# Sending 48 of 2048 softmax score units to VectorE in a two-layer attention and GLU kernel

## The chip, the cores and the metric

The kernel runs on one core of a Trainium2 chip. The metric is the device time of one execution in microseconds; the median of several runs counts. TensorE is called PE, VectorE DVE, ScalarE ACT, GpSimd POOL and SyncE SP, as the profile names them.

## The reference

Two layers of the same two blocks with the same weights, on one sequence of 2048 tokens of width 448. Attention has 16 heads of width 28; the gated block has an inner width of 1792. All arrays are float32.

```python
def _A_ref(x, wqkv, wo):                      # attention
    qkv = (x @ wqkv).reshape(B, S, 3, H, Dh).transpose(2, 0, 3, 1, 4)
    q, k, v = qkv[0], qkv[1], qkv[2]
    scores = einsum("bhqd,bhkd->bhqk", q, k) * (Dh ** -0.5)
    p = softmax(scores, axis=-1)
    o = einsum("bhqk,bhkd->bhqd", p, v)
    return o.transpose(0, 2, 1, 3).reshape(B, S, D) @ wo

def _B_ref(x, w_gate, w_up, w_down):          # gated linear unit
    return (sigmoid(x @ w_gate) * (x @ w_up)) @ w_down

x = A_x
for layer in range(2):
    x = x + _A_ref(layernorm(x), A_wqkv, A_wo)
    x = x + _B_ref(layernorm(x), B_w_gate, B_w_up, B_w_down)
```

## The kernel before

The program is written for one order: the tile framework's own scheduling is off, so every engine executes its instructions in the order in which the Python code issues them. Semaphores are put in where one engine reads what another wrote, or where a buffer is used again. Each layer has four stages: `project` (queries, keys, values), `attend`, `out_project` and `gated`.

The change is in `attend`. Its work is cut into *units*. A unit is one block of 128 keys (`kc`, 16 of them per head) against one block of 512 queries (`qb`, 4 of them). So a head has 64 units, four to a chunk of keys, and a layer has 1024.

- `score(g)` takes the three units of group g. PE writes 3 x 4 matmuls (line 821) into one of two accumulators of three banks each (`triple(g % 2)`); the four matmuls of a unit each fill 32 of the 128 partitions and run side by side. I call these four a *quad*. One ACT instruction (line 828) then takes the exponentials of all 3 x 512 columns into a buffer `prob`, out of a ring of five. A group may start only when ACT has read the group that used the same accumulator, two groups earlier.
- `mix(i)` multiplies half of the queries of one chunk's four units with the values (line 839) and adds them up in `acc`, one bank per head (`bank(h % 2)`). It is two quads on PE. Two of them make up a chunk.
- `finish(h)` runs after a head's last `mix`. DVE copies `acc` out (line 853), spreads and inverts the sum of the exponentials (854, 855), multiplies (856) and splits the result in two halves of 16 bits (857, 858); SP sends it on by DMA (line 871).
- `more(g)` scores group g, and at a head's unit 8 issues the operands of the head after next: a memset on DVE (line 442) and six DMAs on SP.

The loop at the end of `attend` sets PE's order. After each group it lets one or two calls of `mix` follow, alternately, if their exponentials are at least two groups old:

```python
for g in range(2, groups + 3):
    more(g)
    for _ in range(1 + g % 2):
        if i < halves and (NB * (i // 2) + 3) // 3 <= g - 2:
            mix(i)
```

In layer 0 this loop also runs `Prepare`, one step every six chunks: it reads the weights of the later stages, measures them (line 742) and splits them on DVE (lines 183 and 188), and writes them back. Its reads, its writes, the heads' operands and the heads' outputs all go through SP's one queue.

The banks of the accumulators are all in use: two triples, and `bank0` and `bank1` for `acc`. While head h adds up in one of these two, the other holds the sum of head h-1 until line 853 has copied it, and then nothing until head h+1 begins.

Of the kernel before, what the change touches and what calls it, by code (L numbers as in the profile page):

```python
# [11 lines left out]
F32 = mybir.dt.float32  # L12
BF16 = mybir.dt.bfloat16
F16 = mybir.dt.float16
I32 = mybir.dt.int32
AF = mybir.ActivationFunctionType
ALU = mybir.AluOpType
AX = mybir.AxisListType

P = 128  # L20
S = 2048
D = 448
H = 16
DH = 28
F = 1792
NT = S // P
NB = 4
TB = NT // NB
W = TB * P
# [10 lines left out]
VC = 32  # L40
SLACK = 1.0201
GUARD_LIMIT = 56.0

N_SLOTS = 19
N_QUART = 12
# [38 lines left out]
def interleaved_layers(ctx: ExitStack, tc: tile.TileContext, x_in, wqkv, wo, w_gate, w_up,  # L84
                       w_down, out):
    nc = tc.nc
    ctx.enter_context(tc.manual_schedule())

    cpool = ctx.enter_context(tc.tile_pool(name="cpool", bufs=1))
# [4 lines left out]
    qrt = Slots(spool, "q", N_QUART)  # L94
# [4 lines left out]
    def new_banks():  # L99

        if banks["stack"] is not None:
            banks["stack"].close()
        uid[0] += 1
        banks["stack"] = ExitStack()
        banks["pool"] = banks["stack"].enter_context(
            tc.tile_pool(name=f"psum{uid[0]}", bufs=1, space=bass.MemoryType.PSUM,
                         reuse_waits="tile"))

    def psum(tag, name, shape):
        uid[0] += 1  # L110
        return banks["pool"].tile(shape, F32, name=f"{name}_{uid[0]}", tag=tag, bufs=1)

    def triple(i, name):
        return psum(f"triple{i}", name, [P, 3, 512])

    def bank(i, name):
        return psum(f"bank{i}", name, [P, 512])
# [16 lines left out]
    back = cpool.tile([P, 4], F32, name="back")  # L134
# [70 lines left out]
    def both_back(i, a, b, by):  # L205

        e = pw.bitcast(F32)
        nc.vector.scalar_tensor_tensor(back[:, i:i + 1], e[:, a:a + 1], by * 2.0 ** 128,
                                       e[:, b:b + 1], op0=ALU.mult, op1=ALU.mult)
# [172 lines left out]
    class WeightsQKV:  # L382
# [32 lines left out]
        def keep(self):  # L415
            for i in range(2):
                nc.sync.dma_start(qk_parts[i], self.qk[i])
            nc.sync.dma_start(v_parts, self.v)
            big.put(*self.qk, self.v)
# [36 lines left out]
            big.put(self.both)  # L456

    exp_scale = nc.scalar.alloc_register("exp_scale")
    gate_scale = nc.scalar.alloc_register("gate_scale")

    def run_fill(fill, n=1):
# [5 lines left out]
    def project(layer, wq, first):  # L467
# [136 lines left out]
        if layer > 0:  # L604
            big.put(*wq.qk)
        else:
            both_back(0, 0, 1, SCALE * 2.0 ** -20)
            nc.scalar.reg_load(exp_scale, back.bitcast(I32)[0:1, 0:1])

        heads = [HeadOperands(0), HeadOperands(1)]  # L610
        top = cpool.tile([H, 2], F32, name=f"top{layer}", tag="top", bufs=1)
# [20 lines left out]
        def worst_of_heads():  # L632
            pb = bank(4, "bounds")
            nc.tensor.matmul(pb[0:1, 0:H], bnd, ident[0:H, 0:H], start=True, stop=True)
            nc.vector.tensor_reduce(worst, pb[0:1, 0:H], axis=AX.X, op=ALU.max)
            nc.vector.tensor_scalar(flag, worst, back[0:1, 0:1], GUARD_LIMIT / 2, op0=ALU.mult,
                                    op1=ALU.is_gt)
# [162 lines left out]
    def attend(layer, values, heads, last_values, gate, keep):  # L800
        new_banks()
        heads = list(heads)
        outs = Outputs()
        prepare = None
        ring = big.ring(5)
        total = H * NT
        units = total * NB
        probs, accs = {}, {}

        def score(g):  # L810

            ps = triple(g % 2, "sc")
            prob = big.at(ring, "prob", [P, 3, W])
            us = range(3 * g, min(3 * g + 3, units))
            for a, u in enumerate(us):
                c, qb = u // NB, u % NB
                h, kc = c // NT, c % NT
                hd = heads[h]
                for j in range(4):
                    keys = slice(kc * P + 32 * j, kc * P + 32 * j + 32)  # L820
                    nc.tensor.matmul(ps[32 * j:32 * j + 32, a, :], hd.k[:, keys],  # L821
                                     hd.q[:, qb * W:(qb + 1) * W], start=True, stop=True,
                                     tile_position=(0, 32 * j))
                probs[u] = prob[:, a, :]
                if u % (NT * NB) == NT * NB - 1:
                    hd.drop()
            n = len(us)
            nc.scalar.activation(prob[:, 0:n, :], ps[:, 0:n, :], AF.Exp, scale=exp_scale)  # L828

        def mix(i):  # L830

            c, n = i // 2, slice(i % 2 * 256, i % 2 * 256 + 256)
            h, kc = c // NT, c % NT
            if kc == 0 and i % 2 == 0:
                accs[h] = bank(h % 2, "acc")
            acc = accs[h]
            v = values[kc // TB]
            for qb in range(NB):
                nc.tensor.matmul(acc[qb * VC:(qb + 1) * VC, n], v[:, kc % TB, h, :],  # L839
                                 probs[c * NB + qb][:, n], start=(kc == 0 and i % 2 == 0),  # L840
                                 stop=(kc == NT - 1 and i % 2 == 1), tile_position=(0, qb * VC))
            if i % 2:
                for qb in range(NB):
                    probs.pop(c * NB + qb)
                if kc == NT - 1:
                    finish(h)

        def finish(h):
            acc = accs.pop(h)
            raw = qrt.get("oraw", [P, W])  # L850
            den = qrt.get("oden", [P, W])
            hl = qrt.get("ohl", [P, 2, W], F16)
            nc.vector.tensor_copy(raw, acc)  # L853
            nc.vector.stream_shuffle(den, raw, [DH] * 32)
            nc.vector.reciprocal(den, den)  # L855
            nc.vector.tensor_tensor(raw, raw, den, op=ALU.mult)
            nc.vector.tensor_copy(hl[:, 0, :], raw)
            nc.vector.tensor_tensor(hl[:, 1, :], raw, hl[:, 0, :], op=ALU.subtract)
            r, end = h * DH, (h + 1) * DH
            while r < end:  # L860
                kt, p = r // P, r % P
                n = min(P - p, end - r)
                if kt == len(outs.kt):
                    outs.grow()
                o = outs.kt[kt]
                other = nc.scalar if h == H - 1 else nc.sync
                for qb in range(NB):
                    e = qb * VC + r - h * DH
                    c = slice(qb * W, (qb + 1) * W)
                    if kt < 3:  # L870
                        nc.sync.dma_start(o[p:p + n, :, c], hl[e:e + n])
                    else:
                        nc.sync.dma_start(o[p:p + n, c], hl[e:e + n, 0, :])
                        other.dma_start(o[64 + p:64 + p + n, c], hl[e:e + n, 1, :])
                r += n
            qrt.put(raw, den, hl)

        groups = (units + 2) // 3

        def more(g):  # L880
            if g >= groups:
                return
            for u in range(3 * g, 3 * g + 3):
                if u % (NT * NB) == 8:
                    h = u // (NT * NB)
                    if h + 2 < H:
                        hd = HeadOperands(h + 2)
                        heads.append(hd)
                        hd.load()
                        hd.load_guard()  # L890
                    elif h == H - 1:
                        gate.load_out()
                        gate.load_gu()
            score(g)

        for g in range(2):
            more(g)
        last_values()
        halves, i = 2 * total, 0
        for g in range(2, groups + 3):  # L900
            more(g)

            for _ in range(1 + g % 2):
                if i < halves and (NB * (i // 2) + 3) // 3 <= g - 2:
                    mix(i)
                    i += 1
                    c = i // 2 - 1
                    if i % 2:
                        continue
                    if layer == 0 and c == 2:  # L910
                        keep()
                    if layer == 0 and c == 4:
                        prepare = Prepare()
                    if prepare and prepare.steps and c > 4 and c % 6 == 0:
                        prepare.steps.popleft()()
        assert i == halves
        big.put(*values)
        big.free.extend(ring)
        return outs
# [160 lines left out]
    for layer in range(LAYERS):  # L1080
        values, heads, last_values = project(layer, wq, first)
        gate = WeightsGated()
        outs = attend(layer, values, heads, last_values, gate, wq.keep)
        mlp_first = out_project(outs, gate)
        wq = WeightsQKV()

        def before_next(f, wq=wq):
            if f == 6:
                wq.load()

        first = gated(layer, mlp_first, gate, before_next)
# [28 lines left out]
```

## Time and profile before

| | |
|---|---|
| runs | 2023.3, 2023.67, 2027.02 us; median 2023.67 |
| profiled execution | 2026.13 us, its span 2024.2 us, mean granted clock 0.998 |
| PE busy | 2005.5 us (99%) |
| ACT busy | 1189.6 us (59%) |
| DVE busy | 748.8 us (37%) |
| POOL busy | 33.3 us (2%) |
| `attend`, layer 0 | from about 128.9 to 591.2 us |
| `attend`, layer 1 | from about 1129.0 to 1590.9 us |

The busy time of PE is a union of intervals with modelled ends: matmuls overlap each other in it, so 99% doesn't say that PE can't go faster. ACT is busy all through the two `attend` stages and little elsewhere. In the rows of the profile, "x" is the number of instructions, and the two numbers behind the bar are the busy time in microseconds and the mean duration of one in nanoseconds.

### The profile page before, as it was taken

How to read it: one execution, taken by the hardware profiler on the slowest of the kernel's cores; microseconds unless marked ns; L12 is line 12 of the kernel's file. 1: busy time of each engine (PE TensorE's matmuls, PEld its weight loads, DVE VectorE, ACT ScalarE, POOL GpSimd, SP SyncE). 2: the span in 40 equal slices, each digit the busy share in tenths (PEclk: the TensorE clock that was granted, in tenths of full speed). 3: DMA queues.
4: the chain of work that ended last, by engine and by line, in shares of the span. 5: the costliest groups of instructions: out<-in, count | busy, mean ns of one | idle time of the engine just before them, and what ended most of it. 6: DMA issues, size and time to landing. Idle time of an engine off the chain costs nothing. (4 is left out here: it accounts for less than half of the span.)

```text
span 2024.2 us, 47829 instructions
## 1 busy us (share of the span) xinstructions
PE 2005.5 (99%) x21637; PEld 1028.8 (51%) x21637; DVE 748.8 (37%) x1110; ACT 1189.6 (59%) x1136; POOL 33.3 (2%) x75
## 2 busy tenths in 40 slices
PE   8999999999999999999999999999999999999999
PEld 4445555555554444444444555555555544444444
DVE  6635455551235232323274133222322432323222
ACT  5469999999961212121244799999999412121211
POOL 2000000000000000000000000000000000000000
PEclk9999999999999999999999999999999999999999
DMA  4563454741215100001143221121202250101000
GB/s 164 156 195 96 130 157 147 227 131 30 57 59 188 37 13 25 19 19 33 59 130 120 66 66 34 42 46 30 66 12 63 68 204 1 55 1 55 1 19 19
DMA packets 98630, 153.75 MB, mean 76 GB/s; under 512 B 9584, under 2 KB 79216, under 8 KB 95600
## 3 DMA queue, kind: packets, MB, share of 16 engines
q1 hardware_dynamic: 89728, 146.21, 23.9%
q10 hardware_dynamic: 8688, 4.36, 0.8%
q8 instruction: 174, 2.85, 0.6%
q14 instruction: 40, 0.33, 0.1%
HBM read 97.52 MB, written 45.68 MB: 71 GB/s over the span
## 5 line engine op out<-in xcount | busy, mean ns | idle before, releaser
L828 ACT ACTIVATE prob_s<-sc 128x1536 f32<-128x1536 f32 (+1 forms) x684 | 918.2, 1509 | 2.6 <-PE sc L821 1.4
L839 PE MATMUL acc<-prob_s,val_s 128*32 128x256 f32 x8192 | 571.7, 379 | 0.0
L821 PE MATMUL sc<-qp_s 114*32 114x512 f16 x8192 | 569.8, 380 | 1.5 <-ACT val_s L537 1.3
L362 PEld LDWEIGHTS <-gu_s 128*128 128x128 f16 x2464 | 241.1, 98 | 290.4 <-issue 6.4
L839 PEld LDWEIGHTS acc<-prob_s,val_s 128*32 128x32 f32 x8192 | 273.6, 110 | 179.8 <-ACT prob_s L828 0.4
L821 PEld LDWEIGHTS <-qp_s 114*32 114x32 f16 x8192 | 245.8, 95 | 222.3 <-issue 75.8
L362 PE MATMUL gate<-xhl_s,gu_s 128*128 128x512 f16 x1232 | 285.1, 379 | 4.2 <-ACT xhl_s L172 2.6
L362 PE MATMUL up<-xhl_s,gu_s 128*128 128x512 f16 x1232 | 284.2, 379 | 0.0
L1028 ACT ACTIVATE sig_q<-gate 128x512 f32<-128x512 f32 x112 | 66.9, 597 | 341.0 <-PE gate L362 324.8
L1033 DVE SCALAR_TENSOR_TENSOR sig_q<-up,sig_q 128x512 f32<-128x512 f32 x112 | 77.5, 692 | 460.9 <-PE up L362 460.9
L172 ACT CAST hhl_q<-sig_q 128x512 f16<-128x512 f32 x112 | 69.3, 618 | 288.1 <-DVE sig_q L1033 288.1
L853 DVE COPY oraw_q<-acc 128x512 f32<-128x512 f32 x32 | 22.1, 692 | 484.5 <-PE acc L839 484.4
L999 PE MATMUL dnp<-dn_s,hhl_q 128*128 128x448 f16 x448 | 157.9, 352 | 0.0
L998 PE MATMUL dnp<-dn_s,hhl_q 128*128 128x448 f16 x448 | 157.9, 352 | 0.0
L1000 PE MATMUL dnp<-dn_s,hhl_q 128*128 128x448 f16 x448 | 157.9, 352 | 0.0
L362 PE MATMUL qkp<-xhl_s,wqk_s 128*128 128x512 f16 x616 | 140.8, 380 | 0.9 <-DVE xhl_s L178 0.7
L855 DVE RECIPROCAL oden_q<-oden_q 128x512 f32<-128x512 f32 x32 | 107.3, 3353 | 1.1
L173 DVE TENSOR_TENSOR hhl_q<-sig_q,hhl_q 128x512 f16<-128x512 f32 x112 | 77.5, 692 | 76.7 <-ACT hhl_q L172 76.7
L362 PEld LDWEIGHTS <-wqk_s 128*128 128x128 f16 x616 | 57.2, 98 | 71.7 <-issue 4.5
L506 ACT ACTIVATE qkhl_q<-qkp 128x512 f16<-128x512 f32 x56 | 33.4, 596 | 65.5 <-PE qkp L362 65.4
L999 PEld LDWEIGHTS <-hhl_q 128*128 128x128 f16 x448 | 43.8, 98 | 43.8
L998 PEld LDWEIGHTS <-hhl_q 128*128 128x128 f16 x448 | 43.8, 98 | 43.8
(113 smaller groups left out, 1034.8 us busy)
## 6 DMA issues: line engine op xcount, KB each, us to landing
qp_s<-qk_scr SPq DMA_DIRECT2D x96, 224.0 KB
qk_scr<-qkhl_q SPq DMA_DIRECT2D x56, 256.0 KB
gu_s<-gu_parts SPq DMA_DIRECT2D x14, 1024.0 KB
xraw_s<-xt_scr SPq DMA_DIRECT2D x14, 768.0 KB
xt_scr<-xs_s SPq DMA_DIRECT2D x38, 224.0 KB
qp_s<-qk_scr SPq DMA_DIRECT2D x64, 112.0 KB
gu_parts<-pack_s SPq DMA_DIRECT2D x7, 1024.0 KB
raw_s<-in_B_w_down_dram SPq DMA_DIRECT2D x6, 896.0 KB
```

What stands on the lines that cost most here:

```text
L172: nc.scalar.copy(hi, raw)
L173: nc.vector.tensor_tensor(lo, raw, hi, op=ALU.subtract)
L362: nc.tensor.matmul(pm, w, x, start=(i == 0), stop=(i == len(terms) - 1))
L821: nc.tensor.matmul(ps[32 * j:32 * j + 32, a, :], hd.k[:, keys], hd.q[:, qb * W:(qb + 1) * W], start=True, stop=True, tile_position=(0, 32 ...
L828: nc.scalar.activation(prob[:, 0:n, :], ps[:, 0:n, :], AF.Exp, scale=exp_scale)
L839: nc.tensor.matmul(acc[qb * VC:(qb + 1) * VC, n], v[:, kc % TB, h, :], probs[c * NB + qb][:, n], start=(kc == 0 and i % 2 == 0), stop=(kc ...
L855: nc.vector.reciprocal(den, den)
L998: nc.tensor.matmul(pm, hl[:, 0, s], dw[:, 0, :], start=(f == 0), stop=False)
L999: nc.tensor.matmul(pm, hl[:, 0, s], dw[:, 1, :], start=False, stop=False)
L1000: nc.tensor.matmul(pm, hl[:, 1, s], dw[:, 0, :], start=False, stop=(f == NF - 1))
L1028: nc.scalar.activation(sig, pgu[0], AF.Sigmoid, scale=gate_scale)
L1033: nc.vector.scalar_tensor_tensor(sig, pgu[1], PS, sig, op0=ALU.mult, op1=ALU.mult)
```

## The change

In each head, one unit in layer 0 and two units in layer 1 are left out of the groups. Over the kernel that is 16 + 32 = 48 of 2048 units. Each is scored by itself (`score_aside`), ahead of its chunk: into the bank that will be the next head's `acc`, just before the group that holds the first unit of chunk 3 (or of chunk 8, for the second one of layer 1). Ten DVE instructions turn its scores into exponentials as powers of two: multiply by the scale and log2(e) and clamp, add a constant to round, subtract to get the fraction, a polynomial of degree five, a shift of the rounded number into the exponent, and the product. The unit's chunk is 15 in layer 0; in layer 1 it is 10 for the first and 15 for the second.

The groups of three are formed from the units that are left: 336 in layer 0 and 331 in layer 1, where there were 342 in each. The loop that places `mix` is written anew: it goes on while the chunk's last group is at least two groups old and while a proportional pace allows it.

```diff
+        side = {}
+        for h in range(H):
+            for at, kc, qb in ((3, 15, 1),) if layer == 0 else ((3, 10, 3), (8, 15, 1)):
+                side[(h * NT + at) * NB] = (h * NT + kc) * NB + qb
+        main = [u for u in range(units) if u not in side.values()]
+        groups = (len(main) + 2) // 3
+        last_group = {u // NB: n // 3 for n, u in enumerate(main)}
...
-            us = range(3 * g, min(3 * g + 3, units))
+            us = main[3 * g:3 * g + 3]
...
+        def score_aside(u):
+            ps = bank(1 - u // (NT * NB) % 2, "aside")
+            scores(ps, u)
+            y = qrt.get("expo", [P, W])
+            t = qrt.get("whole", [P, W])
+            p = qrt.get("power", [P, W])
+            c = POWER_OF_2
+            nc.vector.tensor_scalar(y, ps, base2[:, 0:1], -126.0, op0=ALU.mult, op1=ALU.max)
+            nc.vector.tensor_scalar(t, y, ROUND, None, op0=ALU.add)
+            nc.vector.scalar_tensor_tensor(y, t, ROUND, y, op0=ALU.subtract, op1=ALU.subtract)
+            nc.vector.tensor_scalar(p, y, c[5], c[4], op0=ALU.mult, op1=ALU.add)
+            nc.vector.tensor_tensor(p, p, y, op=ALU.mult)
+            for k in (3, 2, 1):
+                nc.vector.scalar_tensor_tensor(p, p, c[k], y, op0=ALU.add, op1=ALU.mult)
+            whole = t.bitcast(I32)
+            nc.vector.tensor_scalar(whole, whole, 23, None, op0=ALU.logical_shift_left)
+            nc.vector.scalar_tensor_tensor(p, p, c[0], t, op0=ALU.add, op1=ALU.mult)
...
         def more(g):
             if g >= groups:
                 return
-            for u in range(3 * g, 3 * g + 3):
+            for u in main[3 * g:3 * g + 3]:
+                if u in side:
+                    score_aside(side[u])
...
-            for _ in range(1 + g % 2):
-                if i < halves and (NB * (i // 2) + 3) // 3 <= g - 2:
-                    mix(i)
-                    i += 1
+            while (i < halves and last_group[i // 2] <= g - 2
+                   and (g >= groups or i * groups < halves * (g - 1))):
+                mix(i)
+                i += 1
```

`scores(ps, u)` is the old inner loop of `score`, now a function: four matmuls into a given bank.

More of the change, by code (lines that the diff above doesn't have):

```diff
@@ L42 @@
 GUARD_LIMIT = 56.0
+POWER_OF_2 = (1.0000001192092896, -0.6931469440460205, 0.24022120237350464,
+              -0.05550713464617729, 0.009675540030002594, -0.0013276454992592335)
+ROUND = 12583039.0
 N_SLOTS = 19
@@ L458, in interleaved_layers @@
     exp_scale = nc.scalar.alloc_register("exp_scale")
+    base2 = cpool.tile([P, 1], F32, name="base2")
     gate_scale = nc.scalar.alloc_register("gate_scale")
@@ L608, in project @@
             nc.scalar.reg_load(exp_scale, back.bitcast(I32)[0:1, 0:1])
+            nc.vector.tensor_scalar(base2, back[:, 0:1], math.log2(math.e), None, op0=ALU.mult)
         heads = [HeadOperands(0), HeadOperands(1)]
@@ L808, in attend, with scores @@
         probs, accs = {}, {}
+        side = {}
[5 more added lines that the diff above has]
+        last_group = {u // NB: n // 3 for n, u in enumerate(main)}
+        def scores(ps, u):
+            c, qb = u // NB, u % NB
+            hd, kc = heads[c // NT], c % NT
+            for j in range(4):
+                keys = slice(kc * P + 32 * j, kc * P + 32 * j + 32)
+                nc.tensor.matmul(ps[32 * j:32 * j + 32, :], hd.k[:, keys],
+                                 hd.q[:, qb * W:(qb + 1) * W], start=True, stop=True,
+                                 tile_position=(0, 32 * j))
         def score(g):
@@ L813, in score @@
             prob = big.at(ring, "prob", [P, 3, W])
-            us = range(3 * g, min(3 * g + 3, units))
+            us = main[3 * g:3 * g + 3]
             for a, u in enumerate(us):
[L816 to L823, printed above, removed]
+                scores(ps[:, a, :], u)
                 probs[u] = prob[:, a, :]
                 if u % (NT * NB) == NT * NB - 1:
-                    hd.drop()
+                    heads[u // (NT * NB)].drop()
             n = len(us)
             nc.scalar.activation(prob[:, 0:n, :], ps[:, 0:n, :], AF.Exp, scale=exp_scale)
+        def score_aside(u):
[15 more added lines that the diff above has]
+            nc.vector.scalar_tensor_tensor(p, p, c[0], t, op0=ALU.add, op1=ALU.mult)
+            qrt.put(y, t)
+            probs[u] = p
+            aside.append(u)
+        aside = []
         def mix(i):
@@ L843, in mix @@
                 for qb in range(NB):
-                    probs.pop(c * NB + qb)
+                    p = probs.pop(c * NB + qb)
+                    if c * NB + qb in aside:
+                        qrt.put(p)
                 if kc == NT - 1:
@@ L876, in finish @@
             qrt.put(raw, den, hl)
-        groups = (units + 2) // 3
         def more(g):
@@ L901, in attend @@
             more(g)
-            for _ in range(1 + g % 2):
-                if i < halves and (NB * (i // 2) + 3) // 3 <= g - 2:
-                    mix(i)
-                    i += 1
[L907 to L915, printed above, removed]
+            while (i < halves and last_group[i // 2] <= g - 2
+                   and (g >= groups or i * groups < halves * (g - 1))):
+                mix(i)
+                i += 1
+                c = i // 2 - 1
+                if i % 2:
+                    continue
+                if layer == 0 and c == 2:
+                    keep()
+                if layer == 0 and c == 4:
+                    prepare = Prepare()
+                if prepare and prepare.steps and c > 4 and c % 6 == 0:
+                    prepare.steps.popleft()()
         assert i == halves
```

## The prediction

> **What bounds the kernel now.** I read the page first, then the busy time by stretches, then the timeline of single engines inside `attend`.
>
> ```profile
> PE 2005.5 (99%) x21637; PEld 1028.8 (51%) x21637; DVE 748.8 (37%) x1110; ACT 1189.6 (59%) x1136; POOL 33.3 (2%) x75
> L828 ACT ACTIVATE prob_s<-sc 128x1536 f32<-128x1536 f32 (+1 forms) x684 | 918.2, 1509 | 2.6 <-PE sc L821 1.4
> ```
>
> PE looks full and ACT half idle. The busy time by stretches corrects this for the two `attend` stages (columns: PE, PEld, DVE, ACT, POOL, granted clock, DMA share, GB/s):
>
> ```profile
> 128.90:591.20 462.30, 462.14 (x8204) 260.38 (x8204) 196.04 (x220) 459.72 (x343) 0.45 (x1) 1.00 0.42 123
> 1129.00:1590.90 461.90, 461.77 (x8204) 260.25 (x8204) 122.75 (x120) 459.57 (x343) 0.00 (x0) 1.00 0.18 43
> ```
>
> There ACT is busy for 459.7 of 462.3 us. Which of the two really waits, the timeline shows:
>
> ```profile
> 398.55 14.95 ACT L828 ACTIVATE prob_s<-sc 128x1536 f32<-128x1536 f32 x11
> ...
> 401.24 2.86 ACT L828 ACTIVATE prob_s<-sc 128x1536 f32<-128x1536 f32 x2
> ...
> 401.63 0.84 PE L821 MATMUL sc<-qp_s 114*32 114x512 f16 x12
> 402.28 0.62 PE L839 MATMUL acc<-prob_s,val_s 128*32 128x256 f32 x8
> 402.81 0.83 PE L821 MATMUL sc<-qp_s 114*32 114x512 f16 x12
> 403.45 1.05 PE L839 MATMUL acc<-prob_s,val_s 128*32 128x256 f32 x16
> 404.31 0.84 PE L821 MATMUL sc<-qp_s 114*32 114x512 f16 x12
> ```
>
> Eleven exponentials in 14.95 us with a last one of 1.52 give (14.95 - 1.52) / 10 = 1.343 us per group. PE repeats two groups in 404.31 - 401.63 = 2.68 us, the same pace. In it, every quad takes 0.215 us (404.31 - 403.45 for four), twelve make 2.59, and the rest is one gap: eight mixing matmuls (two quads, 0.44) start at 402.28, and the scores follow only at 402.81. They waited for the ACT instruction that began at 401.24 and ended 1.52 later, at 402.76. So ACT bounds `attend`, but PE is behind it by just 0.09 us in 2.69, or 3.4%.
>
> Three more durations matter. Scores start 0.05 us after ACT has left their accumulator. When ACT is dry, it starts 0.05 after the last score (the third group's scores end at 133.37, ACT stands idle and starts at 133.42) and needs 1.45:
>
> ```profile
> 133.42 1.45 ACT L828 ACTIVATE prob_s<-sc 128x1536 f32<-128x1536 f32 x1 [0.23 <-DMA qp_s<-qk_scr]
> ```
>
> So a dry ACT ends a group 1.50 after its scores; a fed one ends them 1.343 apart.
>
> **The change part by part.**
>
> *Units taken from ACT.* 48 units are 16 groups: 16 x 1.343 = 21.5 us less on ACT (7.2 in layer 0, 14.3 in layer 1).
>
> *DVE's ten instructions.* Nearest rows in layer 0's `attend`:
>
> ```profile
> L858 DVE TENSOR_TENSOR ohl_q<-oraw_q,ohl_q 128x512 f16<-128x512 f32 x15 | 10.4, 692 | 0.5
> L857 DVE CAST ohl_q<-oraw_q 128x512 f16<-128x512 f32 x15 | 6.4, 427 | 0.5
> ```
>
> Seven like the first (two tensors, or from an accumulator) and three like the second (one tensor and constants): 7 x 0.69 + 3 x 0.43 + gaps of 0.03 = 6.4 us; 7.2 if none is like the second. DVE has room: in layer 1 a head's 28.6 us hold `finish` (6.8), a memset (1.8, some 0.5 of waiting) and two of these, 21.9. The tightest use is layer 1's chunk 10. Its power is there about 6.8 + 2.3 + 6.4 = 15.5 us after the last head's copy started; it is mixed ten chunks, 18 us, after. Nothing waits, by 2 to 3 us; the cost is zero.
>
> *PE.* The same quads, in another order. The listing of the changed program shows it. Write S for a group's scores (three quads), M for a whole chunk of mixing (two `mix`, four quads). Before, it runs S M S m (m is half). After, both halves of a chunk become ready at once and the pace never splits them: S S M S M S M, four groups to three chunks. S and M together take 404.31 - 402.81 = 1.51, more than ACT's 1.343, and S S only 0.65. So PE falls behind ACT over three groups and then meets the wait for an accumulator, though the averages are the same. With two accumulators the loop is this. The second S of a pair starts; three S M later (3 x 1.51 = 4.53) the last S of the run starts, its scores end 0.83 later, ACT is dry and ends them 1.50 after that. Three more groups at 1.343 (4.03), 0.05, and the second S of the next pair but one may start: 4.53 + 0.83 + 1.50 + 4.03 + 0.05 = 10.94 us for eight groups, where ACT alone needs 8 x 1.343 = 10.74. Loss: 0.20 per eight groups, 0.525 per head of 21 groups (layer 0), 0.517 per head of 20.67 (layer 1).
>
> To this come, per head, the aside quads (0.215 each, one or two) and runs of five groups with four M instead of three (one per head in layer 0, two in layer 1), each 1.51 - 1.343 = 0.17: at most 0.385 and 0.77, at least nothing where they fall into the half of the loop that runs on ACT. I carried the durations above through the written order of a head: PE starts at the later of its last end and the accumulator's release, ACT ends at the later of its last end + 1.343 and the scores + 1.50. That gives 0.27 and 0.57, so 0.79 and 1.09 us per head in all. Layer 0: 16 x 0.79 - 7.2 = +5.5. Layer 1: 16 x 1.09 - 14.3 = +3.1. Bounds: +1.2 to +7.4 and -6.1 to +6.3.
>
> *The wait for the bank.* Aside scores go to the bank of the last head's sum, so PE now waits for line 853. Between a head's last mixing and the next head's aside, PE has S, S, M (2.2 us; in layer 1 at times S, M, 1.5). The copy mostly ends 0.76 after the last mixing: free. But not behind `Prepare` in layer 0:
>
> ```profile
> 358.55 0.75 DVE L183 TENSOR_SCALAR pack_s<-raw_s,up 128x1024 f16<-128x1024 f32 x1 [10.72 <-DMA dn_parts<-pack_s]
> ...
> 366.00 0.75 DVE L183 TENSOR_SCALAR pack_s<-raw_s,up 128x1024 f16<-128x1024 f32 x1 [3.39 <-DMA raw_s<-in_B_w_gate_dram]
> ...
> 370.53 1.76 DVE L442 MEMSET qp_s<- 18x2048 f16 x1 [0.47 <-issue]
> 372.32 0.69 DVE L853 COPY oraw_q<-acc 128x512 f32<-128x512 f32 x1
> ```
>
> DVE stands in its queue for two DMAs, and the copy of head 7 ends at 373.01, 9.2 us after its last mixing (363.77). Nobody waited; now everything behind PE's aside does. In the changed listing the memset stands behind the copy (1.8 sooner), and head 7 takes 0.35 longer while the DMAs hang on head 6's output: 7.1 late, less 2.2, so PE stands for 4.9 us and ACT with it. Head 8's copy was as late (9.5) but hangs by SP's queue on head 7's output, and PE now comes 4.9 + 0.35 later and the memset goes behind it too: no further wait. The cost: 4.9, from 0 (the DMAs land sooner) to 6.6 (the memset gains nothing).
>
> A PE that stands can also lose clock. The start of the trace shows it: PE idle from 6.95 to 10.08 us, then
>
> ```profile
> 5.00:9.70 4.70, 1.95 (x6) 0.56 (x4) 1.10 (x3) 1.55 (x1) 0.19 (x1) 1.00 1.02 345
> 9.80:16.50 6.70, 5.56 (x22) 4.27 (x23) 4.55 (x14) 2.76 (x6) 5.17 (x15) 0.50 1.09 339
> ```
>
> half the clock for 6.7 us. That would cost half of 6.7, 3.4 us, once; I leave it out of the sum, as 4.9 us is a single wait between dense work, and keep it in the range. The Trainium skill (TensorE: Matmul & The Clock Gate, "What's actually happening") says that one idle window of about 3.4 us, on a free-running count, halves the clock; this trace agrees (3.13 us idle, 0.50). By that rule the wait would hold a whole window about four times in ten, and the sum would then be 3.4 us higher.
>
> *Edits with one answer.* `base2` is one small DVE instruction per kernel; qrt buffers and `last_group` cost nothing; other stages are untouched. Loads of the head after next sit behind `finish` by up to 7 us, with a head (28 us) to spare.
>
> **Sum.** +5.5 + 3.1 + 4.9 = +13.5 us: the profiled execution would go from 2026.13 to 2039.6, the median, 2.5 lower, from 2023.67 to 2037.2.
>
> **The rivals.**
> 1. *ACT stays the bound.* If the runs of three S M are absorbed, the whole 21.5 us show: 2002.2, or 2007.1 with the bank wait. For it: PE has 3.4% to spare on average. Against: 10.94 > 10.74. It decides at 0.20 us per loop: a dry ACT that finished in 1.30 rather than 1.50, or an M shorter by 0.07. Chance 0.13.
> 2. *The loop costs but the aside quads hide and the DMAs land in time:* +1.2 - 6.1 = -4.9, 2018.8; with part of the bank wait about unchanged, near 2021 to 2027. Chance 0.13.
> 3. *DVE falls behind.* In layer 0's heads 3 to 9 the powers push `Prepare` back 6.4 us each, and more copies come late, each by some 5 us: with four, 3 x 4.9 more, 2052. For it: DVE and SP wait for each other there. Against: in the other heads DVE stood idle for 0.8 to 10 us before the copy. Chance 0.12.
>
> That the units do not leave ACT isn't a rival: the listing has 667 exponentials of groups.
>
> **How the numbers follow.** The forecast (loop, most of the quads, one bank wait) has 0.62. A measurement of this kernel tells about 0.2%, 4 us, from no change. Faster: rival 1 and the low end of rival 2, 0.16. Same: the rest of rival 2 and the low end of the forecast, 0.13. Slower: 0.71. The forecast's own bounds are 2018.8 to 2023.67 + 7.4 + 6.3 + 6.6 = 2044; with half clock 2047, and part of rival 3 up to 2050. The range 2018 to 2050 leaves out rival 1 and the top of rival 3.
>
> **What would show it.** In the profile after: ACT no longer busy throughout `attend`, with idle time released by "PE sc" in the last group of each run, about 0.2 us per eight groups; fewer L828 groups (667) at the same 1.343 when fed; S S in PE's timeline; one long PE wait for DVE's copy near head 8 of layer 0, the granted clock beside it; layer 1 about 465 us. It would be wrong if ACT were still busy for all but 2 us of each stage, or if PE waited for a power in mixing.

## The result: 20 us slower, and the profile after

The changed kernel takes 2045.29 us (median of 4 runs, 2044.05 to 2045.78) against 2025.26 for the kernel before in the same comparison: ratio 1.0100, interval 1.0085 to 1.0115. The forecast was 2037.2, 13.5 us slower. The profiled execution took 2044.05, its span 2042.3: 18.1 us more than before.

The page of the changed kernel, the lines that answer to those of before:

```profile
PE 2005.0 (98%) x21637; PEld 1024.8 (50%) x21637; DVE 1039.6 (51%) x1591; ACT 1192.2 (58%) x1119; POOL 33.2 (2%) x75
L846 ACT ACTIVATE prob_s<-sc 128x1536 f32<-128x1536 f32 x667 | 920.7, 1455 | 20.3 <-PE sc L831 11.2
```

ACT's busy time did not fall, though it has 17 instructions fewer. Two things hide in that. The mean of one went from 1509 to 1455 ns: in the kernel before, the rows of a fed ACT overlap (about 1.52 us each, their ends 1.343 apart), so they are longer than they cost; a dry one shows 1.45 us. And the idle time before them went from 2.6 to 20.3 us, 11.2 of it put down to "PE sc": ACT now waits for scores.

The busy time by stretches, the two `attend` stages (columns as before):

```profile
127.90:602.70 474.80, 461.42 (x8189) 258.37 (x8182) 292.29 (x380) 463.73 (x337) 0.45 (x1) 1.00 0.41 120
1140.30:1607.90 467.60, 459.56 (x8192) 257.83 (x8185) 315.62 (x439) 458.00 (x332) 0.00 (x0) 1.00 0.17 42
```

From the first exponential to the end of the last mixing, layer 0 went from 461.3 to 474.7 us (+13.4) and layer 1 from 460.9 to 467.5 (+6.6). That is +20.0; the rest of the span's difference is mostly layer 0's `attend` starting 1.9 us sooner in this execution. DVE is 193 us busier in layer 1, and the profile lists no wait of PE for one of its powers.

Two runs of PE's timeline in layer 1, with ACT beside them:

```profile
1284.80 0.40 PE L881 MATMUL acc<-prob_s,val_s 128*32 128x256 f32 x4
1285.01 0.84 PE L831 MATMUL sc<-qp_s 114*32 114x512 f16 x12
1286.02 0.83 PE L831 MATMUL sc<-qp_s 114*32 114x512 f16 x12 [0.17 <-ACT prob_s L846]
1286.66 1.05 PE L881 MATMUL acc<-prob_s,val_s 128*32 128x256 f32 x16
1287.52 0.84 PE L831 MATMUL sc<-qp_s 114*32 114x512 f16 x12
...
1290.55 0.41 PE L831 MATMUL aside<-qp_s 114*32 114x512 f16 x4
1290.77 0.83 PE L831 MATMUL sc<-qp_s 114*32 114x512 f16 x12
1291.42 1.05 PE L881 MATMUL acc<-prob_s,val_s 128*32 128x256 f32 x16
1292.28 1.77 PE L831 MATMUL sc<-qp_s 114*32 114x512 f16 x24
```

```profile
1289.99 1.45 ACT L846 ACTIVATE prob_s<-sc 128x1536 f32<-128x1536 f32 x1
1291.72 4.31 ACT L846 ACTIVATE prob_s<-sc 128x1536 f32<-128x1536 f32 x3 [0.28 <-PE sc L831]
```

At 1286.02 the second S of a pair waits for ACT; from there S, M, S, M run at 1.51 us a group. At 1290.55 an aside quad adds its 0.215 before the next scores. They end at 1291.60, but ACT has been dry since 1291.44 and starts at 1291.72. Its ends are 1.73 us apart there, where 1.343 is the pace.

The wait for the bank, before head 8 of layer 0 (PE's timeline, then one stretch with the granted clock, the third number from the right):

```profile
366.34 1.05 PE L881 MATMUL acc<-prob_s,val_s 128*32 128x256 f32 x16
370.18 0.40 PE L831 MATMUL aside<-qp_s 114*32 114x512 f16 x4 [2.78 <-DVE oraw_q L897]
```

```profile
371.27:374.68 3.41, 3.41 (x38) 1.71 (x34) 3.38 (x2) 1.98 (x2) 0.00 (x0) 0.50 0.02 5
```

It is the only such wait in the list of PE's waits (the line gives microseconds in total, times, the longest):

```profile
PE aside L831 <- DVE oraw_q L897: 2.8, 1, 2.8
```

PE stood for 2.8 us, and 1.1 us after it had resumed it ran at half clock for 3.41 us, its quads 0.427 us apart instead of 0.215. From the end of one head's mixing to the end of the next, head 8 took 33.9 us where its neighbours took 29.25.

### The profile page after: what moved, and what is told of

Read it like the earlier page. It is cut to its first block, busy times and chain, and to the rows that moved or that the text cites. A ratio compares the mean times of both kernels' runs of the same rounds, so it can differ in the third digit from the quotient of the medians.

```text
span 2042.3 us, 48270 instructions
## 1 busy us (share of the span) xinstructions
PE 2005.0 (98%) x21637; PEld 1024.8 (50%) x21637; DVE 1039.6 (51%) x1591; ACT 1192.2 (58%) x1119; POOL 33.2 (2%) x75
## 5 line engine op out<-in xcount | busy, mean ns | idle before, releaser
L846 ACT ACTIVATE prob_s<-sc 128x1536 f32<-128x1536 f32 x667 | 920.7, 1455 | 20.3 <-PE sc L831 11.2
L831 PE MATMUL sc<-qp_s 114*32 114x512 f16 x8000 | 555.4, 380 | 19.8 <-ACT prob_s L846 9.6
L881 PE MATMUL acc<-prob_s,val_s 128*32 128x256 f32 x8000 | 539.2, 379 | 0.1
L862 DVE SCALAR_TENSOR_TENSOR power_q<-power_q,expo_q 128x512 f32<-128x512 f32 x144 | 99.7, 692 | 4.9
L447 DVE MEMSET qp_s<- 18x2048 f16 x32 | 56.5, 1765 | 23.0 <-issue 14.3
```

The source lines that it names most:

```text
L831: nc.tensor.matmul(ps[32 * j:32 * j + 32, :], hd.k[:, keys], hd.q[:, qb * W:(qb + 1) * W], start=True, stop=True, tile_position=(0, 32 * j))
L862: nc.vector.scalar_tensor_tensor(p, p, c[k], y, op0=ALU.add, op1=ALU.mult)
```

## The experiments

Theory A is the prediction's: the new placing of the mixing makes ACT run dry, and the aside quads push PE further. Theory B: the aside work itself, on PE and DVE, is what costs, whatever the order. Differences are of medians against the kernel before on the same chip; ratios are of the runs compared, with 95% intervals.

**The order alone.** No aside units; the new loop stays.

```diff
-            for at, kc, qb in ((3, 15, 1),) if layer == 0 else ((3, 10, 3), (8, 15, 1)):
+            for at, kc, qb in ():
```

> The changed kernel without any aside unit: all 2048 units are in groups again (342 per layer) and all exponentials are on ACT, but the new loop places the mixing (S S M S M S M). Theory A (the order of the mixing makes ACT run dry): the loop carried through this order with a dry ACT starting 0.113 us after its scores, as the trace of the changed kernel shows, gives +11.1 us per layer against the kernel before, +22 us in all, 2046. Theory B (the aside scores on PE and the powers on DVE cost the time): nothing of it is left, within 3 us of the kernel before.

Measured: 2046.97, +21.6 us, ratio 1.0107 (1.009 to 1.0124). The stages took 473.2 and 472.1 us, +11.9 and +11.2:

```profile
129.80:603.10 473.30, 460.88 (x8189) 257.52 (x8182) 195.67 (x219) 468.69 (x343) 0.45 (x1) 1.00 0.41 120
1141.10:1613.30 472.20, 460.88 (x8195) 257.06 (x8185) 122.05 (x119) 468.19 (x343) 0.00 (x0) 1.00 0.17 42
```

Theory B falls as it stands: with nothing aside, a slowdown of the same size is there. (What the aside work adds of its own is priced below.) Its PE timeline shows the same S S M S M S M:

```profile
1284.03 0.83 PE L831 MATMUL sc<-qp_s 114*32 114x512 f16 x12
1284.68 1.05 PE L881 MATMUL acc<-prob_s,val_s 128*32 128x256 f32 x16
1285.54 0.83 PE L831 MATMUL sc<-qp_s 114*32 114x512 f16 x12
1286.19 1.05 PE L881 MATMUL acc<-prob_s,val_s 128*32 128x256 f32 x16
1287.06 1.78 PE L831 MATMUL sc<-qp_s 114*32 114x512 f16 x24
```

**The aside units with a smoother order.** The pace is held back, so that it, not readiness, decides, and mixing comes in halves again.

```diff
-                   and (g >= groups or i * groups < halves * (g - 1))):
+                   and (g >= groups or i * groups < halves * (g - 2.25))):
```

> The changed kernel with its 48 aside units where they are, but the pace of the mixing held back by 1.25 groups (halves * (g - 2.25) in place of halves * (g - 1)), so that mixing comes in halves again: S M S m. Theory A: about 17 us less than the changed kernel; +1 in layer 0 (-3.6 from the loop, +4.6 bank wait and half clock) and +1.6 in layer 1 (the later last mixing makes some aside scores wait for the bank) against the kernel before, so +3, 2027. Theory B: as slow as the changed kernel, +20.

Measured: 2024.25, -1.1 us, ratio 0.9993 (0.9983 to 1.0003). All of the slowdown is gone by one number. It came out 4 us better than expected. In layer 0 what was expected did show: +0.7 us, with the wait and 3.41 us of half clock from 365.15 on. Layer 1 gave -0.9 where +1.6 was expected, which stays open. PE waits for the copy out of the bank ten times.

```profile
PE aside L831 <- DVE oraw_q L897: 7.6, 10, 2.5
```

**The bank wait alone.** Layer 0's aside at chunk 7 instead of 3, all else as changed.

```diff
-            for at, kc, qb in ((3, 15, 1),) if layer == 0 else ((3, 10, 3), (8, 15, 1)):
+            for at, kc, qb in ((7, 15, 1),) if layer == 0 else ((3, 10, 3), (8, 15, 1)):
```

> The changed kernel with layer 0's aside unit scored ahead of chunk 7 in place of chunk 3, some 7 us later in each head; layer 1 and the order of the mixing as in the change. If the one wait for head 7's copy costs 4.6 us (3.2 us of standing PE and then half clock), 4 to 5 us less than the changed kernel, +15 against the kernel before. Rival (the lost time of that head would be caught up anyway): within 1 us of the changed kernel.

Measured: 2040.24, +14.9 us, ratio 1.0076 (1.0059 to 1.0093). The changed kernel is at +20.0, so the wait with its half clock cost 5 us by the medians. Layer 0's stage fell from 474.7 to 470.4, by 4.3, and its trace has neither the wait nor the half clock.

**Both.** The smoother pace, and every aside where its bank has long been free.

```diff
-            for at, kc, qb in ((3, 15, 1),) if layer == 0 else ((3, 10, 3), (8, 15, 1)):
+            for at, kc, qb in ((7, 15, 1),) if layer == 0 else ((4, 10, 3), (11, 15, 1)):
...
-                   and (g >= groups or i * groups < halves * (g - 1))):
+                   and (g >= groups or i * groups < halves * (g - 2.25))):
```

> Both: the pace held back by 1.25 groups, layer 0's aside at chunk 7, layer 1's at chunks 4 and 11 (used in chunks 10 and 15 as before), so that no aside waits for a bank. Theory A: -4.9 us in layer 0 and -7.7 in layer 1 against the kernel before, -12.6, 2012; not the full -21.5, as PE has 3.4% to spare and the aside scores still push it. Theory B: +15 or more.

Measured: 2012.57, -12.8 us, ratio 0.9938 (0.9921 to 0.9955). It beats both kernels. A second run agrees:

> e4_smooth_and_later once more, in five rounds, beside e8_smooth_plain on the same chip: -12.6 us by the loop, 0.993 to 0.995 of the kernel before.

Measured: 2013.59 against 2024.22, -10.6 us, ratio 0.994 (0.9926 to 0.9953). The stages of the first of the two, by stretches:

```profile
128.50:585.20 456.70, 456.36 (x8189) 261.96 (x8182) 291.61 (x379) 454.82 (x337) 0.45 (x1) 1.00 0.41 124
1122.70:1576.00 453.30, 453.25 (x8192) 264.04 (x8185) 315.71 (x440) 450.08 (x332) 0.00 (x0) 1.00 0.17 43
```

From the first exponential to the last mixing that is 456.7 and 453.2 us, where it was 461.3 and 460.9.

**DVE's ten instructions.** One in place of ten.

```diff
             nc.vector.tensor_scalar(y, ps, base2[:, 0:1], -126.0, op0=ALU.mult, op1=ALU.max)
-            nc.vector.tensor_scalar(t, y, ROUND, None, op0=ALU.add)
...
-            nc.vector.scalar_tensor_tensor(p, p, c[0], t, op0=ALU.add, op1=ALU.mult)
```

(The remaining one writes `p` itself, so the polynomial is left out.)

> The changed kernel with one DVE instruction per aside unit in place of ten: the unit's power is replaced by its clamped, scaled scores (the polynomial is left out). If the ten instructions are hidden, as the prediction has it, within 2 us of the changed kernel, +20 against the kernel before. Rival (DVE's work delays the copy out of the bank or the mixing): several us less, up to the 4.6 us of the bank wait in layer 0.

Measured: 2045.57, +19.3 us, ratio 1.0093 (1.0076 to 1.011); the changed kernel was at +20.0. Nine instructions times 48 cost nothing that can be measured here. Layer 1, which holds 32 of the 48 units and has no wait for the bank, took 467.4 us against 467.5. In layer 0 the wait for the bank was longer in this execution, with less work on DVE:

```profile
PE aside L831 <- DVE oraw_q L888: 4.0, 1, 4.0
```

**The aside quads.** From the run with the later bank, the scores of the aside units are taken out, and all of their DVE work but one memset: the 48 units count as ones.

```diff
-            ps = bank(1 - u // (NT * NB) % 2, "aside")
-            scores(ps, u)
...
+            nc.vector.memset(p, 1.0)
```

> The changed kernel, layer 0's aside at chunk 7, with no aside scores on PE and no powers on DVE: the 48 units get ones (their scores and exponentials are left out). Compared with e3_bank_later (+14.9) it prices the 48 aside quads and DVE's work together. The loop carried through its order, with a dry start of 0.113 us, gives -3.4 us in layer 0 and -6.4 in layer 1 for the missing quads: +5 against the kernel before. If the quads were hidden, +15; if even their bare 48 x 0.215 = 10.3 us came out, +4.6. It stays above the kernel before, although ACT has 21.5 us less to do, if the order is what costs.

Measured: 2030.65, +4.4 us, ratio 1.0022 (1.0012 to 1.0031). Against the +14.9 with them, the 48 quads cost 10.5 us (DVE's work cost nothing, as the run before this one showed): about their bare 48 x 0.215 = 10.3. The stages of the profiled executions give 3.4 and 6.4, 9.8 in all. In this order PE's time is on the path and nothing hides them. And with ACT relieved of 21.5 us and PE of 10.3, the kernel is still slower than before: the order takes all that ACT gained.

**Two units per head in layer 0 as well.** The change is against the kernel of "Both".

```diff
-            for at, kc, qb in ((7, 15, 1),) if layer == 0 else ((4, 10, 3), (11, 15, 1)):
+            for at, kc, qb in ((7, 13, 3), (10, 15, 1)) if layer == 0 else ((4, 10, 3), (11, 15, 1)):
```

> e4_smooth_and_later with two aside units per head in layer 0 as well (at chunks 7 and 10, used in chunks 13 and 15): 64 units in all. The loop gives -6.5 us in layer 0 in place of -4.9, so -14.2 against the kernel before, 2011, if DVE keeps up. Rival: DVE, busy in layer 0 with the weights of later stages, is late with the powers or the copies in heads 3 to 9, and it is slower than e4_smooth_and_later by 2 us or more.

Measured: 2026.57, +0.3 us, ratio 1.0003 (0.9994 to 1.0013). The rival holds: 13 us are lost again, all in layer 0 (469.6 us against 456.7; layer 1 stays at 453.2). PE's waits name DVE:

```profile
PE acc L881 <- DVE power_q L865: 5.0, 3, 3.4
PE aside L831 <- DVE expo_q L856: 4.7, 3, 3.3
```

Mixing waits for a power, and a second aside for the bank that the first still fills, three times each, the longest 3.4 us. These are 9.7 of the 13 us. The clock would account for the rest: after the two longest waits it was half for 3.41 us each, and half of 2 x 3.41 is 3.4 (columns as before).

```profile
333.22:336.62 3.40, 2.82 (x28) 1.28 (x32) 2.88 (x4) 0.36 (x1) 0.00 (x0) 0.50 0.44 117
411.73:415.12 3.39, 2.83 (x28) 1.35 (x31) 3.22 (x6) 0.81 (x1) 0.00 (x0) 0.50 0.73 192
```

**Is the gain the new pace's?** No aside units, with the pace held back.

```diff
-            for at, kc, qb in ((3, 15, 1),) if layer == 0 else ((3, 10, 3), (8, 15, 1)):
+            for at, kc, qb in ():
...
-                   and (g >= groups or i * groups < halves * (g - 1))):
+                   and (g >= groups or i * groups < halves * (g - 2.25))):
```

> No aside units, all 2048 in groups, but the mixing held back by 1.25 groups as in e4_smooth_and_later: is the gain of that run the aside units' or the new pace's? Theory A: the old kernel was bound by ACT's 1.343 us per group throughout, and no order makes that shorter: +0.1 us by the loop, within 2 us of the kernel before. Rival (the order before had a loss of its own, and the new pace alone gains): several us faster than the kernel before.

Measured: 2035.55, +11.3 us, ratio 1.0054 (1.004 to 1.0068): a miss for both theories. The trace shows why. In each layer every fourth group from 219 to 339 ends about 0.158 us late, 31 in all; those are just the groups whose buffer of the ring of five is read by a mixing that stands behind their own scores on PE. 31 x 0.158 = 4.9 us per layer, 9.8 of the 11.3. So this was no clean control, and the next one is:

```diff
-                   and (g >= groups or i * groups < halves * (g - 2.25))):
+                   and (g >= groups or i * groups < halves * (g - 2))):
```

> No aside units, the mixing held back by one group in place of 1.25. In e8_smooth_plain 31 groups per layer (219, 223 and so on to 339) lost 0.158 us each: the last mixing that reads the buffer five groups back stands behind their scores on PE, so their exponential waits for it. At one group no such group is left. Theory A (order alone sets the loss; ACT bounds the rest): within 2 us of the kernel before. Rival (the new pace costs by itself): +11 as e8_smooth_plain.

Measured: 2025.14, -0.75 us, ratio 0.9996 (0.9987 to 1.0005). With all units in groups, the new loop is as fast as the old one at this pace, and slower at the pace of the best version. So the 11 to 13 us of the best version come with the units that were moved to DVE: at neither pace did the loop gain anything without them. (The best version itself was not run at this pace.)

## Why the prediction was right, point by point

- *What bounds the kernel.* Right. ACT bounded `attend` with PE 3.4% behind; a version that puts both in a good order gains, and an order that doesn't feed ACT loses.
- *The loop S S M S M S M.* Right as a mechanism (e1_order_alone), too small in size. The term "a dry ACT ends a group 1.50 after its scores" took the start 0.05 us after the last score from one row, the third group of the stage. The dry starts of the changed kernel come 0.112 after (1291.606 to 1291.718), as one late start did in the trace of before (0.105, at 147.16). With 0.06 more the same walk through the order gives +8.5 in layer 0 and +6.4 in layer 1 instead of +5.5 and +3.1. Layer 1 measured +6.6; layer 0 +13.4, or 8.7 without the 4.65 of head 8. These 6.3 us are nearly the whole of the 6.5 between forecast (+13.5) and result (+20.0).
- *Aside quads and runs of five.* Put at 0.27 and 0.57 us per head, 13.4 us in all. The quads alone are worth 10.5 (e6_no_aside_scores). The walk through the order sized them well; the lower bound, that they hide, is wrong for this order, and rival 2 falls with it.
- *The bank wait.* Right in head and cause: line 897 behind `Prepare`'s splits, before head 8, once. Put at 4.9 us; PE began the aside 5.2 us after head 7's last mixing, and not 2.26 after as in most heads of layer 0, so it lost 3.0 (the profile calls 2.78 of them idle). The DMAs that held DVE landed sooner against it: the copy ended 5.2 late, not 7.1.
- *The clock.* I left the half clock out of the sum, and it came. Head 8 took 33.9 - 29.25 = 4.65 us too long, so 4.65 - 3.0 = 1.7 are the clock's: half of the 3.41 us. Taken into the sum at the 3.4 us of the start of the trace, the clock would have been twice too dear: that half clock had lasted 6.7 us. Two errors cancelled, by luck: 4.9 was forecast, 4.65 came.
- *DVE.* Right. The ten instructions of an aside took 6.37 us from start to end (6.4 forecast), no mixing waited for them in the changed kernel, and their removal changed nothing (e5_one_dve_step). Rival 3 did not happen here; e7_two_per_head shows how near it was.
- *Rival 1*, the full 21.5 us, fell. Even the best order shows 11 to 13 of them. Its stages took 456.7 and 453.2 us, where the groups alone are 336 x 1.343 = 451 and 331 x 1.343 = 445 on ACT. In its trace most of the late exponentials are again dry starts, 0.11 us after their scores; no run was made to find what takes the rest. PE's busy time (456.4 of 456.7 us) doesn't tell, as it was 462.1 of 462.3 when ACT was the bound.

Together: 8.5 + 4.65 + 6.4 = 19.6 by the corrected terms, 20.0 by the stages.

## What to carry to other kernels

When two engines are within a few per cent of each other, their order decides more than their work: the same totals, with mixing issued by whole chunks instead of halves, cost 21 us, and one number in the pace turned +20 into -1. Before work is taken from the bounding engine, carry the start and release times of both through the written order, with the latency of a *dry* engine, read from rows that wait as those of the changed kernel will. And a buffer that is "idle" is free only when its last reader is: look at what that reader's queue is behind.

## What the runs showed of the hardware

- In the changed kernel some 200 dry starts of ACT come 0.106 to 0.118 us after the last matmul; in the third group of each stage it is 0.05. In the former an event instruction of 17 ns on ACT's queue, which waits for PE, stands between the two (at 1291.651, after scores that ended at 1291.606 and before a start at 1291.718); in the third groups none does, and the exponential waits for PE itself. The Trainium skill (Perfetto Trace Analysis, "Identifying Dependency Chains") says that instructions which wait for several engines may get such event instructions ahead of them; the trace agrees, with 689 of them for line 846. That they make the 0.06 us is only argued; no run took them away.
- ACT's own pace on 1536 columns: 1.45 us alone, 1.343 between ends when fed, while the rows in the kernel before read 1.52 in the median. Such rows overlap; the distance of the ends tells the pace.
- 2.8 us of standing PE (matmuls end at 367.39, the aside starts at 370.18) cost half the clock for 3.41 us, from 371.27 on. I had thought 4.9 us of waiting too short to matter. In the traces of all runs, each of the five waits of PE of 2 us or more in `attend` was followed by 3.41 us of half clock: 2.78 here, 2.47 (e2_smooth_order), 4.0 (e5_one_dve_step), 3.42 and 3.27 (e7_two_per_head). The Trainium skill (TensorE: Matmul & The Clock Gate, "What's actually happening"), which the prediction cites, asks for an idle window of about 3.4 us; here 2.47 were enough, so these traces don't agree with it to the letter. Nor do the 3.13 us at the start of the trace, which the prediction took for agreement.
